# A first transform in two column tiles of 64, with the product x times v folded on VectorE alone

## The chip, the core and the metric

The kernel runs on one core of a Trainium2 chip. The metric is device time in microseconds (us) from launch to end. PE is TensorE, ACT ScalarE, DVE VectorE, POOL GpSimd; SP is the queue that issues most DMAs. 1 GB/s is a thousand bytes per us.

## What is computed

A long convolution, a gate and two MLPs in sequence, over 12,480 positions of 128 channels, all in float32:

```python
h_filt = (np.maximum(pos_emb @ w1, 0.0) @ w2) * np.exp(-0.01 * pos)[:, None]
u = x * v
y = irfft(rfft(u, n=2*S) * rfft(h_filt, n=2*S), n=2*S)[:S]      # S = 12480
a = x * y
b = np.maximum(a @ w_in, 0.0) ** 2 @ w_out                      # 128 -> 2048 -> 128
h = b @ w_in2
out = (h / (1 + np.exp(-1.702 * h))) @ w_out2
```

## The kernel before

The convolution is a transform of length 99 x 127, done as matmuls. The sequence is laid out with 99 rows on the partitions and 127 columns, and the columns are paired around the middle one: a sum and a difference of columns j and -j, 64 of each (`NJ`), so 128 values per row and channel.

*Filter stage* (`filter_stage`). PE computes the hidden layer (tile `hp`), VectorE applies relu and window (tile `r`, L264), and sum and difference go to `h`: sums on GpSimd (L268, the last on VectorE), differences on VectorE (L270).

*Product and fold* (`Inputs`). x and v come in 16 chunks of 8 channels (`load`, L196 and L197: 96 rows and 3 rows of each, so four DMAs a chunk, on SP). GpSimd multiplies x by v in two halves (L207). The sum of the paired columns (`even`, L215) is GpSimd's for even chunks and VectorE's for odd ones, the difference (`odd`, L225) VectorE's. Both fill `u`, a ring of 7 tiles.

*First transform* (`s1_step`). 16 steps over `h` fill `G`, then 32 steps over `u` fill `A`, four channels a step. PE multiplies each channel's 99 x 128 block by the cosines and sines of `cs1` (L280) into a PSUM bank, of which there are four. The lower 64 partitions (from sums) are copied as they are; the upper 64 (from differences) need real and imaginary part exchanged and one sign turned. Two steps of three are evicted by ACT (L288 to L290), the third by VectorE (L284, L286). After each step `advance` multiplies, folds and loads chunks by a table of steps (`odds`); chunk c is used in steps 2c and 2c + 1 of A.

*Around it.* After steps 6, 10, 14 and 18 of A the ACT queue writes a quarter of `G` to DRAM (`gd`, L666). From step 25 on `w2b` and the first five `m` tiles are loaded on SP (L672, L299), after steps 26 and 28 the first two pieces of `gd` are read back as `Gs` on the ACT queue (L306); these use memory that the chunks' buffers occupied. The second stage then begins with `fk` (L328), and after it the MLPs, which are most of the time.

The order on each engine is as written (`tc.manual_schedule`). A DMA's issue signals one of eight semaphores, taken in turn (`DMAHW0` to `DMAHW7`); an issue that takes a semaphore again first waits until the DMA that had it has landed.

Of the kernel before, what the change touches and what calls it, by code (L numbers as in the profile page):

```python
# [9 lines left out]
FP32 = mybir.dt.float32  # L10
# [3 lines left out]
ACTF = mybir.ActivationFunctionType  # L14
# [19 lines left out]
XC = 8  # L34
# [57 lines left out]
def conv_mlp_kernel(ctx: ExitStack, tc: tile.TileContext, xc, xt, vc, pt, w1, w2,  # L92
# [4 lines left out]
    const = ctx.enter_context(tc.tile_pool(name="const", bufs=1))  # L97
    dram = ctx.enter_context(tc.tile_pool(name="dram", bufs=1, space=bass.MemoryType.DRAM))

    cs1 = const.tile([N1, 2 * N1], FP32, name="cs1")  # L100
    ci2 = const.tile([N1, 2, N1], FP32, name="ci2")
    sign = const.tile([128, 2], FP32, name="sign")

    bd = dram.tile([2, NJ, N1, 2, D], FP32, name="bd")
    gd = dram.tile([128, N1, 2 * F], FP32, name="gd")
# [74 lines left out]
    class Inputs:  # L180


        def __init__(self, up, pool, first, early):
            self.up, self.pool, self.tiles, self.u = up, pool, {}, {}
            self.first, self.early = first, early
            self.loaded = self.done = self.odd_done = 0

        def load(self):
            c = self.loaded
            if c == NXC or c >= self.early and c - max(self.odd_done, self.early) == 3:  # L190
                return
            self.loaded += 1
            pool, bufs = (self.first, self.early) if c < self.early else (self.pool, 3)
            xs, vs = (pool.tile([N1, XC, 2, NJ], FP32, tag=n, name=n, bufs=bufs) for n in ("x", "v"))
            for r in (slice(0, ROWS), slice(ROWS, N1)):
                nc.sync.dma_start(out=xs[r], in_=xc[c, r])  # L196
                nc.sync.dma_start(out=vs[r], in_=vc[c, r])  # L197
            self.tiles[c] = xs, vs

        def multiply(self):  # L200
            c = self.done
            if c == self.loaded:
                return
            self.done += 1
            xs, vs = self.tiles[c]
            for i in range(0, XC, 4):
                nc.gpsimd.tensor_tensor(out=xs[:, i:i + 4], in0=xs[:, i:i + 4], in1=vs[:, i:i + 4],  # L207
                                        op=ALU.mult)
            self.u[c] = self.up.tile([N1, XC, 2 * NJ], FP32, tag="u", name="u", bufs=7)
            if c % 2 == 0:  # L210
                self.even(c, nc.gpsimd)

        def even(self, c, engine):
            xs, _ = self.tiles[c]
            engine.tensor_tensor(out=self.u[c][:, :, 0:NJ], in0=xs[:, :, 0], in1=xs[:, :, 1], op=ALU.add)  # L215

        def odd(self):
            c = self.odd_done
            if c == self.done:
                return  # L220
            self.odd_done += 1
            if c % 2:
                self.even(c, nc.vector)
            xs, _ = self.tiles.pop(c)
            nc.vector.tensor_tensor(out=self.u[c][:, :, NJ:2 * NJ], in0=xs[:, :, 0], in1=xs[:, :, 1],  # L225
                                    op=ALU.subtract)

    def filter_stage(fp, bank, h, inputs):

        HC = 4  # L230
        NC_ = NJ // HC
        bw1 = fp.tile([128, 128], FP32, name="bw1", bufs=1)
        warm = fp.tile([128, 1], FP32, name="warm", bufs=1)
        win = fp.tile([N1, 2, NJ], FP32, name="win", bufs=1)
        nc.vector.memset(warm, 0.0)
        p_t = {}

        def load_pos(c):
            p = fp.tile([128, HC, N1], FP32, tag="pos", name="pos", bufs=12)
            nc.sync.dma_start(out=p, in_=pt[:, c * HC:(c + 1) * HC, :])  # L240
            p_t[c] = p

        nc.scalar.dma_start(out=bw1, in_=w1)
        for c in range(12):
            load_pos(c)
        nc.scalar.dma_start(out=win, in_=c_win)
        nc.scalar.activation(out=warm, in_=warm, func=ACTF.Sigmoid)
        nc.scalar.dma_start(out=cs1, in_=c_s1)
        nc.vector.memset(sign[:, 0:1], 1.0)
        nc.vector.memset(sign[:, 1:2], -1.0)  # L250

        for j in range(0, NJ, JF):
            for c in range(j // HC + 12, min(j // HC + 12 + JF // HC, NC_)):
                load_pos(c)
            if j >= JF:
                inputs.load()
            ps = bank("hp")[:N1]
            for i in range(JF):
                nc.tensor.matmul(out=ps[:, i * 2 * F:(i + 1) * 2 * F],
                                 lhsT=p_t[(j + i) // HC][:, (j + i) % HC, :], rhs=bw1)  # L260
            r = fp.tile([N1, 2, F, JF], FP32, tag="r", name="r")
            for s in range(2):
                wb = win[:, s, j:j + JF].unsqueeze(1).to_broadcast([N1, F, JF])
                nc.vector.scalar_tensor_tensor(  # L264
                    out=r[:, s], in0=ps.rearrange("p (j s f) -> p s f j", j=JF, s=2)[:, s],
                    scalar=0.0, in1=wb, op0=ALU.max, op1=ALU.mult)
            last = j + JF == NJ
            (nc.vector if last else nc.gpsimd).tensor_tensor(  # L268
                out=h[:, :, j:j + JF], in0=r[:, 0], in1=r[:, 1], op=ALU.add)
            nc.vector.tensor_tensor(out=h[:, :, NJ + j:NJ + j + JF], in0=r[:, 0], in1=r[:, 1],  # L270
                                    op=ALU.subtract)
            if j >= NJ - 2 * JF:
                inputs.multiply()

    def s1_step(bank, src, d, dst, on_vector):


        ps = bank("s1").rearrange("p (e k) -> p e k", e=4)[:, :, 0:2 * N1]
        for e in range(4):
            nc.tensor.matmul(out=ps[:, e], lhsT=src[:, d + e, :], rhs=cs1)  # L280
        ps = ps.rearrange("p e (c k) -> p k c e", c=2)
        low, high = slice(0, NJ), slice(NJ, 128)
        if on_vector:
            nc.vector.tensor_copy(out=dst[low], in_=ps[low])  # L284
            sb = sign[high].unsqueeze(1).unsqueeze(3).to_broadcast([NJ, N1, 2, 4])
            nc.vector.tensor_tensor(out=dst[high], in0=ps[high, :, ::-1], in1=sb, op=ALU.mult)  # L286
        else:
            nc.scalar.copy(out=dst[low], in_=ps[low])  # L288
            nc.scalar.copy(out=dst[high, :, 0], in_=ps[high, :, 1])
            nc.scalar.activation(out=dst[high, :, 1], in_=ps[high, :, 0], func=ACTF.Copy, scale=-1.0)  # L290

    m_t, h_t = {}, {}

# [333 lines left out]
    with tc.manual_schedule():  # L627
# [7 lines left out]
        G = sgs.enter_context(tc.tile_pool(name="G", bufs=1, side="right")).tile(  # L635
            [128, N1, 2, F], FP32, name="G")
        vp = vps.enter_context(tc.tile_pool(name="v", bufs=3, side="right"))
        odds = {-(-12 * c // 5) + 1 for c in range(NXC)}
        steps = [0]

        def advance():
            inputs.multiply()
            if steps[0] in odds:
                inputs.odd()
            inputs.load()
            steps[0] += 1

        with tc.tile_pool(name="h", bufs=1) as hp:
            h = hp.tile([N1, F, 2 * NJ], FP32, name="h")
            inputs = Inputs(up, vp, hp, 5)  # L650
            with tc.tile_pool(name="fil", bufs=2) as fp:
                filter_stage(fp, bank, h, inputs)
            for f in range(0, F, 4):
                s1_step(bank, h, f, G[:, :, :, f:f + 4], f // 4 % 3 == 2)
                advance()
            assert inputs.odd_done >= inputs.early
        with tc.tile_pool(name="A", bufs=1, reuse_waits="tile") as ap_, ExitStack() as mps:
            A = ap_.tile([128, N1, 2, D], FP32, name="A")
            for d in range(0, D, 4):
                s1_step(bank, inputs.u[d // XC], d % XC, A[:, :, :, d:d + 4], d // 4 % 3 == 2)  # L660
                if d // 4 < 25:
                    advance()
                if d // 4 in (6, 10, 14, 18):
                    q = 25 * (d // 16 - 1)
                    q = slice(q, min(q + 25, N1))
                    nc.scalar.dma_start(out=gd[:, q], in_=G[:, q].rearrange("p k c f -> p k (c f)"))  # L666
                if d // 4 == 25:
                    assert inputs.odd_done == NXC
                    vps.close()
                    mp = mps.enter_context(tc.tile_pool(name="mh", bufs=1, reuse_waits="tile"))  # L670
                    w2b = mp.tile([128, 2 * D], FP32, name="w2b")
                    nc.sync.dma_start(out=w2b, in_=w2)  # L672
                if d // 4 in (25, 26, 27, 28, 29):
                    load_m(mp, d // 4 - 25)
                if d // 4 in (26, 28):
                    load_h(mp, (d // 4 - 26) // 2)
            sgs.close()
# [15 lines left out]
def _constants():  # L693
# [6 lines left out]
        return 2.0 * np.pi * ((num % den) / den)  # L700

    a = angle(n1[:, None] * (4 * k1[None, :] + 1), 4 * N1)
    s1 = np.concatenate([np.cos(a), -np.sin(a)], 1)
    i2 = np.stack([np.cos(a.T) / NT, -np.sin(a.T) / NT], 1)
    a = angle(j[:, None, None] * (4 * (k1[None, :, None] + N1 * k2[None, None, :]) + 1), 4 * NT)
    s2 = np.zeros((128, N1, 2, 128))
# [72 lines left out]
```

## Time and profile before

| | |
|---|---|
| median of 3 runs | 1455.44 us (1452.51 to 1455.81) |
| the profiled execution | 1450.28 us |
| its span, first to last instruction | 1448.5 us |
| granted TensorE clock, mean | 0.986 of full speed |
| PE busy | 1410.4 us (97%) |
| VectorE, ACT, GpSimd busy | 1128.7, 956.9, 278.7 us |
| chain that ended last | PE 88%, VectorE 4%, DMA 4% |

The shares are means over stages with different limits. The diff touches the first 121 us alone, so this stretch has to be read by itself. A matmul in float32 leaves two records in the trace, and a weight load (PEld) beside each.

### The profile page before, as it was taken

How to read it: one execution, taken by the hardware profiler on the slowest of the kernel's cores; microseconds unless marked ns; L12 is line 12 of the kernel's file. 1: busy time of each engine (PE TensorE's matmuls, PEld its weight loads, DVE VectorE, ACT ScalarE, POOL GpSimd, SP SyncE). 2: the span in 40 equal slices, each digit the busy share in tenths (PEclk: the TensorE clock that was granted, in tenths of full speed). 3: DMA queues.
4: the chain of work that ended last, by engine and by line, in shares of the span. 5: the costliest groups of instructions: out<-in, count | busy, mean ns of one | idle time of the engine just before them, and what ended most of it. 6: DMA issues, size and time to landing. Idle time of an engine off the chain costs nothing.

```text
span 1448.5 us, 17134 instructions
## 1 busy us (share of the span) xinstructions
PE 1410.4 (97%) x6634; PEld 1193.6 (82%) x6634; DVE 1128.7 (78%) x1241; ACT 956.9 (66%) x1117; POOL 278.7 (19%) x249
## 2 busy tenths in 40 slices
PE   7888999999999999999999999999999999999998
PEld 7877888788878888888888888888888888888887
DVE  6736898779987778777777777777787777877887
ACT  1654444376766777767676667777777667777776
POOL 7651222234622100121011210112001120000000
PEclk9999999999999999999999999999999999999999
DMA  9395776522210000100000000000000000000000
GB/s 257 90 299 176 238 245 211 180 81 78 74 37 19 26 26 8 37 19 26 17 18 30 26 26 8 26 30 27 26 8 26 30 26 8 8 8 0 15 15 14
DMA packets 46397, 91.21 MB, mean 63 GB/s; under 512 B 4183, under 2 KB 30604, under 8 KB 45804
## 3 DMA queue, kind: packets, MB, share of 16 engines
q1 hardware_dynamic: 35886, 57.17, 13.5%
q10 hardware_dynamic: 10430, 32.95, 5.9%
q8 instruction: 52, 0.85, 0.2%
q14 instruction: 29, 0.24, 0.1%
HBM read 64.25 MB, written 25.85 MB: 62 GB/s over the span
## 4 chain that ended last, share of the span: by engine, by line
PE 88%; DVE 4%; DMA 4%; issue 2%; ACT 1%; POOL 1%; SPq 0%; POOLq 0%; DVEq 0%; ACTq 0%
PE hin L512 12%; PE hin L511 12%; PE hin L513 12%; PE acc L512 12%; PE acc L511 12%; PE acc L513 12%; PE yps L469 4%; PE s L280 3%; PE hk L339 3%; PE xk L341 3%; PE ob L365 3%; PE fk L328 2%; DMA gd<-G 1%; DVE gl L549 1%; DMA m<-in_c_s_dram 1%
## 5 line engine op out<-in xcount | busy, mean ns | idle before, releaser
L549 DVE TENSOR_TENSOR gl<-g,gh 128x1004 fp32r<-128x1004 f32 (+4 forms) x400 | 491.4, 1229 | 35.1 <-ACT gh L545 34.5
L529 ACT ACTIVATE g<-hin 128x1004 f32<-128x1004 f32 (+4 forms) x200 | 201.2, 1006 | 237.9 <-PE hin L513 237.3
L511 PE MATMUL acc<-gh,w 128*128 128x502 f32 (+4 forms) x800 | 313.5, 392 | 0.4 <-DVE lo L458 0.4
L511 PE MATMUL hin<-hi,w 128*128 128x502 f32 (+4 forms) x800 | 312.7, 391 | 0.0
L512 PE MATMUL acc<-gl,w 128*128 128x502 f32 (+4 forms) x800 | 311.8, 390 | 0.8 <-DVE gl L549 0.8
L512 PE MATMUL hin<-lo,w 128*128 128x502 f32 (+4 forms) x800 | 312.3, 390 | 0.0
L513 PE MATMUL acc<-gh,w 128*128 128x502 f32 (+4 forms) x800 | 311.7, 390 | 0.0
L513 PE MATMUL hin<-hi,w 128*128 128x502 f32 (+4 forms) x800 | 311.5, 389 | 0.0
L416 POOL TENSOR_TENSOR b<-uv 99x256 f32<-99x256 f32 x127 | 159.6, 1286 | 699.0 <-DMA uv<-bd 508.5
L540 DVE TENSOR_TENSOR g<-hin,g 128x1004 f32<-128x1004 f32 (+4 forms) x200 | 238.7, 1193 | 50.6 <-ACT g L532 50.6
L538 DVE CAST gh<-g 128x1004 fp32r<-128x1004 f32 (+4 forms) x200 | 141.6, 708 | 150.8 <-ACT g L530 150.8
L532 ACT ACTIVATE g<-hin 128x1004 f32<-128x1004 f32 (+4 forms) x200 | 200.1, 1000 | 75.2 <-PE hin L513 67.2
L530 ACT ACTIVATE g<-g 128x1004 f32<-128x1004 f32 (+4 forms) x200 | 208.0, 1040 | 6.4
L545 ACT CAST gh<-g 128x1004 fp32r<-128x1004 f32 (+4 forms) x200 | 202.8, 1014 | 0.4 <-DVE g L540 0.4
L511 PEld LDWEIGHTS hin<-hi,w 128*128 128x128 f32 x800 | 151.3, 189 | 33.9 <-ACT g L529 2.4
L512 PEld LDWEIGHTS acc<-gl,w 128*128 128x128 f32 x800 | 151.0, 189 | 31.9 <-DVE gl L549 2.0
L513 PEld LDWEIGHTS hin<-hi,w 128*128 128x128 f32 x800 | 151.3, 189 | 30.7
L511 PEld LDWEIGHTS acc<-gh,w 128*128 128x128 f32 x800 | 151.1, 189 | 31.0 <-DVE lo L458 0.9
L512 PEld LDWEIGHTS hin<-lo,w 128*128 128x128 f32 x800 | 151.3, 189 | 30.6 <-issue 0.5
L513 PEld LDWEIGHTS acc<-gh,w 128*128 128x128 f32 x800 | 150.8, 189 | 30.4
L352 DVE TENSOR_TENSOR t<-xk,hc 128x512 f32<-128x512 f32 (+1 forms) x100 | 63.8, 679 | 25.8 <-PE xk L341 13.9
L469 PEld LDWEIGHTS yps<-ci,b 99*128 99x128 f32 x508 | 62.7, 196 | 8.2 <-issue 2.8
(67 smaller groups left out, 1132.5 us busy)
## 6 DMA issues: line engine op xcount, KB each, us to landing
uv<-bd SPq DMA_DIRECT2D x64, 198.0 KB
m<-in_c_s_dram SPq DMA_DIRECT2D x49, 256.0 KB
bd<-bs ACTq DMA_DIRECT2D x24, 512.0 KB
x<-in_xc_dram SPq DMA_DIRECT2D x16, 384.0 KB
v<-in_vc_dram SPq DMA_DIRECT2D x16, 384.0 KB
Gs<-gd ACTq DMA_DIRECT2D x12, 512.0 KB
gd<-G ACTq DMA_DIRECT2D x3, 1600.0 KB
raw<-in_moe_w_in_dram SPq DMA_DIRECT2D x8, 512.0 KB
```

The costliest lines, as they stand in the source:

```text
L416: engine.tensor_tensor(out=b[:, :, s, c], in0=uv[:, 0, :, c], in1=uv[:, 1, :, 1 - c], op=ALU.add if s != c else ALU.subtract)
L469: nc.tensor.matmul(out=ps[:, o:o + w], lhsT=b[:, c, :], rhs=ci2[:, c, r:r + w], start=(c == 0), stop=(c == 1))
L511: nc.tensor.matmul(out=out, lhsT=a, rhs=hl[0], start=first, stop=False)
L512: nc.tensor.matmul(out=out, lhsT=a, rhs=hl[1], start=False, stop=False)
L513: nc.tensor.matmul(out=out, lhsT=b, rhs=hl[0], start=False, stop=last)
L529: nc.scalar.activation(out=g, in_=ps, func=ACTF.Relu)
L530: nc.scalar.activation(out=g, in_=g, func=ACTF.Square)
L532: nc.scalar.activation(out=g, in_=ps, func=ACTF.Sigmoid, scale=1.702)
L538: nc.vector.tensor_copy(out=gh, in_=g)
L540: nc.vector.tensor_tensor(out=g, in0=ps, in1=g, op=ALU.mult)
L545: nc.scalar.copy(out=gh, in_=g)
L549: nc.vector.tensor_tensor(out=gl, in0=g, in1=gh.bitcast(FP32), op=ALU.subtract)
```

## The change

Each channel's matmul is cut in two: the 64 sum columns and the 64 difference columns of a channel are weights of a matmul each (`src[:, d + e, j]`), the first to output partitions 0 to 63, the second to 64 to 127. The program marks them as tiles of 128 rows by 64 columns, at columns 0 and 64. `cs1` gets a second pair of columns with exchange and sign built in, so that one ACT copy evicts all 128 partitions; VectorE evicts nothing. The product is one VectorE instruction a chunk, the two halves of the fold two more, all in `fold`; GpSimd does nothing for `u`. The table of steps changes with it: a chunk from 7 on is folded three steps of A after the ring's older tile has been used, and `w2b` and `m` are asked for from step 22 on.

```diff
-    cs1 = const.tile([N1, 2 * N1], FP32, name="cs1")
+    cs1 = const.tile([N1, 2, 2 * N1], FP32, name="cs1")
...
-            if c == NXC or c >= self.early and c - max(self.odd_done, self.early) == 3:
+            if c == NXC or c >= self.early and c - max(self.done, self.early) == 3:
...
-        def multiply(self):
+        def fold(self):
             c = self.done
             if c == self.loaded:
                 return
             self.done += 1
-            xs, vs = self.tiles[c]
-            for i in range(0, XC, 4):
-                nc.gpsimd.tensor_tensor(out=xs[:, i:i + 4], in0=xs[:, i:i + 4], in1=vs[:, i:i + 4],
-                                        op=ALU.mult)
-            self.u[c] = self.up.tile([N1, XC, 2 * NJ], FP32, tag="u", name="u", bufs=7)
-            if c % 2 == 0:
-                self.even(c, nc.gpsimd)
...
+            xs, vs = self.tiles.pop(c)
+            u = self.u[c] = self.up.tile([N1, XC, 2 * NJ], FP32, tag="u", name="u", bufs=7)
+            nc.vector.tensor_tensor(out=xs, in0=xs, in1=vs, op=ALU.mult)
+            nc.vector.tensor_tensor(out=u[:, :, 0:NJ], in0=xs[:, :, 0], in1=xs[:, :, 1], op=ALU.add)
+            nc.vector.tensor_tensor(out=u[:, :, NJ:2 * NJ], in0=xs[:, :, 0], in1=xs[:, :, 1],
                                     op=ALU.subtract)
...
-            if j >= NJ - 2 * JF:
-                inputs.multiply()
-
-    def s1_step(bank, src, d, dst, on_vector):
+
+    def s1_step(bank, src, d, dst):
...
         for e in range(4):
-            nc.tensor.matmul(out=ps[:, e], lhsT=src[:, d + e, :], rhs=cs1)
-        ps = ps.rearrange("p e (c k) -> p k c e", c=2)
-        low, high = slice(0, NJ), slice(NJ, 128)
-        if on_vector:
-            nc.vector.tensor_copy(out=dst[low], in_=ps[low])
-            sb = sign[high].unsqueeze(1).unsqueeze(3).to_broadcast([NJ, N1, 2, 4])
-            nc.vector.tensor_tensor(out=dst[high], in0=ps[high, :, ::-1], in1=sb, op=ALU.mult)
-        else:
-            nc.scalar.copy(out=dst[low], in_=ps[low])
-            nc.scalar.copy(out=dst[high, :, 0], in_=ps[high, :, 1])
-            nc.scalar.activation(out=dst[high, :, 1], in_=ps[high, :, 0], func=ACTF.Copy, scale=-1.0)
+            for half in range(2):
+                j = slice(half * NJ, (half + 1) * NJ)
+                nc.tensor.matmul(out=ps[j, e], lhsT=src[:, d + e, j], rhs=cs1[:, half])
+        nc.scalar.copy(out=dst, in_=ps.rearrange("p e (c k) -> p k c e", c=2))
...
-        odds = {-(-12 * c // 5) + 1 for c in range(NXC)}
+        folds = {max(-(-11 * c // 5) + 1, 2 * c + 4 if c >= 7 else 0) for c in range(NXC)}
...
-            inputs.multiply()
-            if steps[0] in odds:
-                inputs.odd()
+            if steps[0] in folds:
+                inputs.fold()
...
-                if d // 4 < 25:
+                if d // 4 < 22:
                     advance()
...
-                if d // 4 == 25:
-                    assert inputs.odd_done == NXC
+                if d // 4 == 22:
+                    assert inputs.done == NXC
...
-                if d // 4 in (25, 26, 27, 28, 29):
-                    load_m(mp, d // 4 - 25)
+                if 22 <= d // 4 < 27:
+                    load_m(mp, d // 4 - 22)
...
-    s1 = np.concatenate([np.cos(a), -np.sin(a)], 1)
+    s1 = np.stack([np.concatenate([np.cos(a), -np.sin(a)], 1),
+                   np.concatenate([-np.sin(a), -np.cos(a)], 1)], 1)
```

VectorE's queue from the last filter block on, first before: the folds (`u`) stand between evictions (`G<-s1`) that wait for PE.

```order
L264 SCALAR_TENSOR_TENSOR r_282<-hp_273,win_89 99x512
L268 TENSOR_TENSOR h_83<-r_282 99x64x8 [waits DVE_49]
L270 TENSOR_TENSOR h_83<-r_282 99x64x8
L225 TENSOR_TENSOR u_265<-x_143 99x8x64 [waits DMAHW5_49,DMAHW3_49,Pool_49]
L284 COPY G_76<-s1_321 64x198x4 [waits PE_49]
L286 TENSOR_TENSOR G_76<-s1_321,sign_62 64x198x4
L215 TENSOR_TENSOR u_289<-x_163 99x8x64 [waits DMAHW7_49,DMAHW1_49,Pool_49]
L225 TENSOR_TENSOR u_289<-x_163 99x8x64
L284 COPY G_76<-s1_357 64x198x4 [waits PE_49]
```

And now, at the same place (L206 to L208 are `fold`, `x_140` is chunk 0):

```order
L245 SCALAR_TENSOR_TENSOR r_275<-hp_266,win_88 99x512
L249 TENSOR_TENSOR h_82<-r_275 99x64x8 [waits DVE_49]
L251 TENSOR_TENSOR h_82<-r_275 99x64x8
L206 TENSOR_TENSOR x_140<-x_140,v_141 99x1024 [waits DMAHW5_49,DMAHW6_49,DMAHW4_49,DMAHW3_49]
L207 TENSOR_TENSOR u_307<-x_140 99x8x64 [waits DVE_49]
L208 TENSOR_TENSOR u_307<-x_140 99x8x64
L206 TENSOR_TENSOR x_160<-x_160,v_161 99x1024 [waits DMAHW2_49,DMAHW7_49,DMAHW1_49,DMAHW0_49]
L207 TENSOR_TENSOR u_341<-x_160 99x8x64 [waits DVE_49]
L208 TENSOR_TENSOR u_341<-x_160 99x8x64
```

The evictions have gone from it, and the product stands ahead of each fold.

SP's queue, before, from the last piece of chunk 9 (`x_474`, `v_475`) to the first of chunk 11 (`x_534`); `x_500` and `v_501` are chunk 10:

```order
L197 DMA v_475<-in_vc_dram 3x1024 [waits DMAHW3_49]
L196 DMA x_500<-in_xc_dram 96x1024 [waits DMAHW4_49,DVE_49,Pool_49]
L197 DMA v_501<-in_vc_dram 96x1024 [waits DMAHW5_49,DMAHW0_49]
L196 DMA x_500<-in_xc_dram 3x1024 [waits DMAHW6_49]
L197 DMA v_501<-in_vc_dram 3x1024 [waits DMAHW0_49]
L196 DMA x_534<-in_xc_dram 96x1024 [waits DMAHW1_49,DVE_49,Pool_49]
```

And now, from the last piece of chunk 8 (`v_442`) over chunk 9 (`x_481`, `v_482`) and chunk 10 (`x_526`, `v_527`) to the third piece of chunk 11 (`x_556`, `v_557`):

```order
L196 DMA v_442<-in_vc_dram 3x1024 [waits DMAHW0_49]
L195 DMA x_481<-in_xc_dram 96x1024 [waits DMAHW1_49,DVE_49]
L196 DMA v_482<-in_vc_dram 96x1024 [waits DMAHW2_49]
L195 DMA x_481<-in_xc_dram 3x1024 [waits DMAHW3_49]
L196 DMA v_482<-in_vc_dram 3x1024 [waits DMAHW4_49]
L195 DMA x_526<-in_xc_dram 96x1024 [waits DMAHW7_49,DMAHW6_49,DVE_49]
L196 DMA v_527<-in_vc_dram 96x1024 [waits DMAHW7_49]
L195 DMA x_526<-in_xc_dram 3x1024 [waits DMAHW0_49]
L196 DMA v_527<-in_vc_dram 3x1024 [waits DMAHW1_49]
L195 DMA x_556<-in_xc_dram 96x1024 [waits DMAHW2_49,DVE_49]
L196 DMA v_557<-in_vc_dram 96x1024 [waits DMAHW5_49,DMAHW4_49]
L195 DMA x_556<-in_xc_dram 3x1024 [waits DMAHW5_49]
```

The first write of `G` signals `DMAHW0` before and `DMAHW1` now (ACT's rows below). Before, the last piece of chunk 10 waited for it; now the first piece of chunk 9 does. The second write (`DMAHW7`) is waited for by chunk 10's v, the third (`DMAHW5`) by chunk 11's third piece.

ACT's queue around that first write, before:

```order
L288 COPY A_464<-s1_540 64x198x4 [waits PE_49]
L289 COPY A_464<-s1_540 64x99x4
L290 ACTIVATE A_464<-s1_540 64x99x4
L666 DMA gd_64<-G_76 128x3200 [waits DMAHW0_49,DVE_49,Activation_49]
L288 COPY A_464<-s1_552 64x198x4 [waits PE_49]
L289 COPY A_464<-s1_552 64x99x4
```

And now, to the second write:

```order
L262 COPY A_491<-s1_572 128x198x4 [waits PE_49]
L637 DMA gd_63<-G_75 128x3200 [waits DMAHW1_49,Activation_49]
L262 COPY A_491<-s1_593 128x198x4 [waits PE_49]
L262 COPY A_491<-s1_603 128x198x4 [waits PE_49]
L262 COPY A_491<-s1_623 128x198x4 [waits PE_49]
L262 COPY A_491<-s1_633 128x198x4 [waits PE_49]
L637 DMA gd_63<-G_75 128x3200 [waits DMAHW7_49]
```

One copy a step has taken the place of three instructions; the first write still follows step 6 of A, the second step 10. The end of the transform on ACT, before (from the copy of step 26, with the two reads of `Gs`):

```order
L288 COPY A_464<-s1_742 64x198x4 [waits PE_49]
L289 COPY A_464<-s1_742 64x99x4
L290 ACTIVATE A_464<-s1_742 64x99x4
L306 DMA Gs_767<-gd_64 128x1024 [waits DMAHW3_49,DMAHW5_49,DMAHW2_49,DMAHW6_49,DMAHW0_49,DMAHW7_49,DVE_49,Pool_49]
L288 COPY A_464<-s1_769 64x198x4 [waits PE_49]
L289 COPY A_464<-s1_769 64x99x4
L290 ACTIVATE A_464<-s1_769 64x99x4
L288 COPY A_464<-s1_779 64x198x4 [waits PE_49]
L289 COPY A_464<-s1_779 64x99x4
L290 ACTIVATE A_464<-s1_779 64x99x4
L306 DMA Gs_789<-gd_64 128x1024 [waits DMAHW7_49,DMAHW6_49]
L288 COPY A_464<-s1_800 64x198x4 [waits PE_49]
```

And now:

```order
L262 COPY A_491<-s1_842 128x198x4 [waits PE_49]
L278 DMA Gs_854<-gd_63 128x1024 [waits DMAHW4_49,DMAHW3_49,DMAHW5_49,DMAHW2_49,DMAHW6_49,DMAHW1_49,DMAHW7_49,DMAHW0_49,DVE_49]
L262 COPY A_491<-s1_856 128x198x4 [waits PE_49]
L262 COPY A_491<-s1_866 128x198x4 [waits PE_49]
L278 DMA Gs_876<-gd_63 128x1024 [waits DMAHW6_49,DMAHW4_49]
L262 COPY A_491<-s1_878 128x198x4 [waits PE_49]
L262 COPY A_491<-s1_888 128x198x4 [waits PE_49]
L262 COPY A_491<-s1_898 128x198x4 [waits PE_49]
L303 COPY fs_936<-fk_931 128x512 [waits DMAHW6_49,DMAHW4_49,PE_49]
```

The first `Gs` stands where it stood, but five steps' copies are behind it now, where VectorE had one of them before.

## Rows read from the trace of the kernel before

**Rows 1.** Windows: start:end, length, busy PE PEld DVE ACT POOL, PEclk, DMA share, GB/s.

```profile
14.00:38.00 24.00, 18.02 (x110) 17.84 (x109) 18.21 (x21) 6.79 (x12) 23.25 (x17) 0.86 0.98 245
...
78.00:100.00 22.00, 17.39 (x80) 16.65 (x81) 9.70 (x12) 11.34 (x21) 13.65 (x10) 0.84 1.00 330
100.00:121.00 21.00, 14.23 (x67) 12.74 (x65) 9.98 (x12) 10.83 (x20) 6.72 (x5) 0.84 0.69 210
131.00:200.00 69.00, 68.48 (x360) 61.32 (x359) 60.84 (x92) 34.55 (x60) 19.87 (x23) 1.00 0.69 230
```

**Rows 2.** Chain of waits, 64 to 122 us: start, us, what.

```profile
68.46 8.74 DMA gd<-G
...
91.81 7.11 DMA gd<-G
...
99.64 6.37 DMA v<-in_vc_dram
...
106.45 2.49 POOL x L207 x2
...
108.96 0.69 DVE u L215
109.65 0.61 DVE u L225
...
120.98 1.05 PE fk L328 x7
```

**Rows 3.** Groups by form, 20 to 125 us: count, busy us and mean ns, idle before.

```profile
L288 ACT COPY A<-s 64x792 f32<-64x792 f32 x22 | 17.9, 812 | 23.4 <-PE s L280 17.4 <-DVE u L225 5.7
...
L290 ACT ACTIVATE A<-s 64x396 f32<-64x396 f32 x22 | 10.9, 495 | 0.0
...
L286 DVE TENSOR_TENSOR A<-s,sign 64x792 f32<-64x792 f32 x10 | 9.9, 985 | 0.1
L284 DVE COPY A<-s 64x792 f32<-64x792 f32 x10 | 9.8, 975 | 6.1 <-issue 4.7 <-PE s L280 1.1
```

**Rows 4.** Timeline, 20 to 70 us, start of the transform: start, us, engine, line.

```profile
22.35 1.66 DVE L268 TENSOR_TENSOR h<-r 99x512 f32<-99x512 f32 x1
...
23.92 1.75 DVE L270 TENSOR_TENSOR h<-r 99x512 f32<-99x512 f32 x1
...
25.82 17.77 PE L280 MATMUL s<-cs,h 99*128 99x198 f32 x88 [5.98 <-DVE h L270]
...
28.83 0.81 ACT L288 COPY G<-s 64x792 f32<-64x792 f32 x1 [25.49 <-PE s L280]
...
31.47 0.81 ACT L288 COPY G<-s 64x792 f32<-64x792 f32 x1 [0.93 <-PE s L280]
```

**Rows 5.** Timeline of ACT, 66 to 72.5 us: first copies three steps apart.

```profile
68.38 0.81 ACT L288 COPY A<-s 64x792 f32<-64x792 f32 x1 [0.58 <-PE s L280]
...
72.40 0.81 ACT L288 COPY A<-s 64x792 f32<-64x792 f32 x1 [0.58 <-PE s L280]
```

**Rows 6.** The page's groups: ACT reading PSUM on 128 partitions.

```profile
L529 ACT ACTIVATE g<-hin 128x1004 f32<-128x1004 f32 (+4 forms) x200 | 201.2, 1006 | 237.9 <-PE hin L513 237.3
```

**Rows 7.** VectorE's groups by form: two inputs from SBUF on 128 partitions.

```profile
L549 DVE TENSOR_TENSOR gl<-g,gh 128x1004 fp32r<-128x1004 f32 x176 | 219.1, 1245 | 19.7 <-ACT gh L545 19.3
```

**Rows 8.** Chain of waits, 0 to 150 us: short matmuls back to back.

```profile
124.81 0.89 PE fk L328 x8
```

**Rows 9.** DMA issues, 0 to 130 us: count, KB each.

```profile
x<-in_xc_dram SPq DMA_DIRECT2D x16, 384.0 KB
...
gd<-G ACTq DMA_DIRECT2D x3, 1600.0 KB
```

**Rows 10.** Timeline of SP, 66 to 79 us: first and last piece of chunk 10.

```profile
67.99 0.32 SPq L196 DMA_DIRECT2D x<-in_xc_dram  x1
...
77.22 0.25 SPq L197 DMA_DIRECT2D v<-in_vc_dram  x1
```

**Rows 11.** Waits, 24 to 121 us: total, times, longest.

```profile
ACT A L288 <- DVE u L225: 5.7, 1, 5.7
```

More of the change, by code (lines that the diff above doesn't have):

```diff
@@ L98, in conv_mlp_kernel @@
     dram = ctx.enter_context(tc.tile_pool(name="dram", bufs=1, space=bass.MemoryType.DRAM))
-    cs1 = const.tile([N1, 2 * N1], FP32, name="cs1")
+    cs1 = const.tile([N1, 2, 2 * N1], FP32, name="cs1")
     ci2 = const.tile([N1, 2, N1], FP32, name="ci2")
-    sign = const.tile([128, 2], FP32, name="sign")
     bd = dram.tile([2, NJ, N1, 2, D], FP32, name="bd")
@@ L185, in __init__ @@
             self.first, self.early = first, early
-            self.loaded = self.done = self.odd_done = 0
+            self.loaded = self.done = 0
         def load(self):
             c = self.loaded
-            if c == NXC or c >= self.early and c - max(self.odd_done, self.early) == 3:
+            if c == NXC or c >= self.early and c - max(self.done, self.early) == 3:
                 return
@@ L204, in multiply @@
             self.done += 1
-            xs, vs = self.tiles[c]
-            for i in range(0, XC, 4):
-                nc.gpsimd.tensor_tensor(out=xs[:, i:i + 4], in0=xs[:, i:i + 4], in1=vs[:, i:i + 4],
-                                        op=ALU.mult)
-            self.u[c] = self.up.tile([N1, XC, 2 * NJ], FP32, tag="u", name="u", bufs=7)
-            if c % 2 == 0:
-                self.even(c, nc.gpsimd)
[L213 to L225, printed above, removed]
+            xs, vs = self.tiles.pop(c)
[3 more added lines that the diff above has]
+            nc.vector.tensor_tensor(out=u[:, :, NJ:2 * NJ], in0=xs[:, :, 0], in1=xs[:, :, 1],
                                     op=ALU.subtract)
@@ L248, in filter_stage @@
         nc.scalar.dma_start(out=cs1, in_=c_s1)
-        nc.vector.memset(sign[:, 0:1], 1.0)
-        nc.vector.memset(sign[:, 1:2], -1.0)
         for j in range(0, NJ, JF):
@@ L653, in conv_mlp_kernel @@
             for f in range(0, F, 4):
-                s1_step(bank, h, f, G[:, :, :, f:f + 4], f // 4 % 3 == 2)
+                s1_step(bank, h, f, G[:, :, :, f:f + 4])
                 advance()
-            assert inputs.odd_done >= inputs.early
+            assert inputs.done >= inputs.early
         with tc.tile_pool(name="A", bufs=1, reuse_waits="tile") as ap_, ExitStack() as mps:
@@ L659, in conv_mlp_kernel @@
             for d in range(0, D, 4):
-                s1_step(bank, inputs.u[d // XC], d % XC, A[:, :, :, d:d + 4], d // 4 % 3 == 2)
-                if d // 4 < 25:
+                s1_step(bank, inputs.u[d // XC], d % XC, A[:, :, :, d:d + 4])
+                if d // 4 < 22:
                     advance()
```

## The prediction

> **What bounds the kernel now.** I read the windows by stage first, for PE's busy time, clock and the share of the DMA engines; then the chain of waits over the stage that the diff touches; then that stage's groups by form. From 131 us on PE is busy 68.48 us of 69 [rows 1], in code that the change leaves alone: nothing is to be won there. From 78 to 121 us, the second half of the first transform, it is busy 17.39 of 22 us and 14.23 of 21 us, at a mean granted clock of 0.84, while the DMA engines are full (share 1.00, 330 GB/s) [rows 1]. The chain there is no arithmetic: it stands in the write of G to DRAM (8.74 and 7.11 us), in the last piece of a v (6.37 us), and after that in GpSimd's product (2.49 us) and VectorE's fold (0.69 and 0.61 us) [rows 2]. So the touched stage lasts from PE's first `s1` matmul at 25.82 us [rows 4] to `fk` at 120.98 us [rows 2]: 95.2 us for 48 steps.
>
> Where nothing waits, ACT's first copies of steps three apart start at 68.38 and 72.40 us [rows 5]: 1.34 us a step, or 167.5 ns for each of a step's 8 matmul records (an fp32 matmul leaves two). 48 such steps are 64.3 us; the other 31 us of the stage are waits and lower clock. That is all that this change can win.
>
> **The change part by part.**
>
> *Eviction.* ACT's three instructions (0.81 us, and two halves of some 0.5 us, of which the last is shown) or VectorE's two (0.98 and 0.99 us) [rows 3] become one ACT copy of 128 x 792. The trace has that copy on 64 partitions, 0.81 us [rows 3], and a 128-partition read of PSUM with 1,004 elements at 1,006 ns [rows 6], about 1 ns an element either way; bounds 0.79 and the 1.8 us that the three take now, taken 0.81. It hides behind PE's 1.34 us a step; were that cover gone, 48 copies would cost 39 us. VectorE no longer evicts, so a fold that waits for data no longer holds up an eviction queued behind it.
>
> *Product and fold.* 16 folds of one 99 x 1,024 product and two 99 x 512 operations. A VectorE operation of the same kind on 128 x 1,004 takes 1,245 ns [rows 7], the two halves 0.69 and a further 0.61 us [rows 2]: 1.25 + 0.69 + 0.61 = 2.55 us a chunk, 41 us in all, beside PE's 64 (and on the path only where PE waits for a chunk). Next to a working GpSimd such a half takes 1.75 us [rows 4], which bounds a fold at some 6.5 us; GpSimd has nothing left to do in this stage, so I take 2.55. That quiet also shortens the last two `h` operations, 1.66 and 1.75 us [rows 4], to 0.69 each: PE starts 2.0 us earlier, at 23.8 us. From then on a chunk's GpSimd time (2.49 us) is off the path.
>
> *Small things.* Two memsets go and `cs1` doubles; both lie in the filter stage, before 23.8 us; uncovered, the 77 KB more would cost 0.3 us at 245 GB/s [rows 1]. [...]
>
> *The matmuls.* 8 a step instead of 4, each with all 198 moving columns but 64 weight columns, alternately on the lower and upper half of the output partitions. No row shows such a pair. If the two halves run side by side, a step stays at 1.34 us (no less, since each record still streams 198 columns); if they run one after the other, it is 16 x 167.5 ns = 2.68 us. I take 1.34: the trace shows loads of weights running under matmuls already (8 records of 128 columns with their loads in 0.89 us [rows 8], 111 ns each), so neither load nor issue has been the limit down to that rate, and the halves share no weights and no output partition. [...]
>
> [...]
>
> *DMA.* Each chunk is 2 x 384 KB (0.8 MB with its small pieces), G's writes 1,600 KB each [rows 9], 6.5 MB in all. A DMA's issue waits for the earlier DMA that used its semaphore. Now chunk 10's first piece is issued at 67.99 us, its last only at 77.22 [rows 10], when the first write of G (issued 68.46, 8.74 us) has landed [rows 2]. In the new order chunk 9's first piece takes over the semaphore of that write, a chunk earlier; chunk 10 then has the second write's, chunk 11 the third's, chunk 13 the fourth's. On SP everything behind waits too: the later chunks, `w2b`, the `m` tiles. VectorE's fold waits for them, then PE; on VectorE only later folds stand behind.
> The first write follows step 6 of A: 23.8 + 2.7 + 23 x 1.34 + 0.8 = 58.1 us. From there 6.5 MB of G and 7 chunks (5.7 MB) must move. In the kernel before, 6.5 MB and 6 chunks (4.9 MB) took from 68.46 to 106.0 us [rows 2]: 302 GB/s. 12.2 MB at that rate are 40.3 us: the last chunk lands at 98.4 us. (330 GB/s [rows 1] would give 95, and is the low end; a wait for each write in turn is a rival.)
> Then its fold, 2.55: 101.0. The read-back `Gs` stands on ACT ahead of the last five copies and waits for the last fold: it did so before, when ACT stood 5.7 us for VectorE's fold [rows 11]. Issue 0.4, five copies 4.1, the second issue 0.4 (PE's last two steps, 2.7, lie beside these, or 5.4 at the lower clock): about 106 to 107, taken 107. Before, the same tail from the last landing took 15 us, with GpSimd's product and the lower clock in it.
>
> **Sum.** 120.98 - 107 = 14 us off. Of the profiled execution's 1450.28 us (span 1448.5 and 1.8 around it) that leaves 1436.3. Its runs' median is 1455.44, 5.2 above that execution, so I name **1441.4 us**. A measurement of this kernel tells about 0.3% (4.4 us) from no change.
>
> **Rivals.**
>
> *One after the other* (the other sign). The two halves share the 198-column stream or the issue, and PE needs 2.68 us a step. For it: no row shows two matmuls at once, and every dense stretch goes exactly by columns. Against it: different partitions of the output, different weight columns. Time: 23.8 + 2.7 + 128.6 + 1 = 156 us for `fk`, DMA far from binding: +35, 1490 us. It decides from 1.95 us a step on, where (121 - 27.5)/48 eats the whole stage.
>
> *Loads exposed.* Weights of the other half are not fetched until the matmul ahead of them has begun, so a half's matmul starts one load late. A load costs at most 111 ns for 128 columns [rows 8]; half the columns, 56 to 111. A step is then 8 x (167.5 + 56 to 111) = 1.78 to 2.23 us. At 1.78 the first write of G comes at about 67 us, the DMA work ends at 107.5 and `fk` comes at 115: 6 us won, 1449; at 2.23 PE ends at 134: 13 us lost, 1468. [...]
>
> *The chunks take it all back.* If each of the four writes must land alone before the chunk behind it moves, 4 x 8 us and 7 chunks of 3.3 us (0.8 MB at 245 GB/s, the rate while chunks alone moved [rows 1]) take 55 us from 58.1: `fk` at 121, nothing won, 1455. For it: the four held pieces. Against: the trace moves chunks beside writes at 330 GB/s [rows 1].
>
> **How the numbers follow.** Forecast 0.52 (own range 1431 to 1449: `fk` from 97 to 115), loads exposed 0.23, one after the other 0.17, chunks 0.08. The serial case and the ends of the forecast are left out: about 0.2 lie outside 1430 to 1466, which takes in all but the slowest exposed loads. Faster by over 0.3%: nearly all of the forecast and half of the exposed loads, 0.62; within 0.3%: the chunks and the middle of the exposed loads, 0.15; slower: the serial case and slow loads, 0.23.
>
> **What the profile after would show.** Two matmul records of different halves begun within one record's time, and copies 1.34 us apart, prove the tiling; 1.8 or 2.7 apart name the rival. Six or more us between the first write of G and chunk 9's issue on SP prove the held chunk; PE then waits on VectorE's folds from A's step 18 on. `fk` should start near 107 us and PE from there on run as before. Wrong would be: a step over 1.95 us, folds slower than 3 us, or PE's clock falling in the waits for chunks, which would stretch the last steps.

## The result and the profile after

| | before | after | ratio, 95% interval |
|---|---|---|---|
| median, 4 runs each | 1453.97 us | 1434.91 us (1431.45 to 1438.78) | 0.9873 (0.9838 to 0.9907) |
| repeated later, 9 and 5 runs | 1450.29 us | 1435.67 us (1433.29 to 1438.28) | 0.9889 (0.9868 to 0.9909) |
| profiled execution | 1450.28 us | 1431.45 us | |
| `fk` starts, profiled execution | 120.98 us | 105.00 us | |

The changed kernel is 1.1 to 1.3% faster. The touched stage ends 16.0 us earlier. The profiled executions differ by 18.8 us; the other 2.8 us lie behind `fk`, in code that is the same: from `fk` to the end of the span 1324.7 us against 1327.5. In the repeat it was 1330.0 us, so that part is spread between executions.

Windows of the stage after the change (columns as in [rows 1]):

```profile
24.00:45.00 21.00, 21.00 (x251) 18.03 (x252) 18.41 (x23) 12.05 (x15) 0.00 (x0) 1.00 0.91 220
45.00:55.00 10.00, 10.00 (x124) 8.59 (x122) 3.72 (x5) 5.96 (x8) 0.00 (x0) 1.00 0.01 2
55.00:60.50 5.50, 5.50 (x70) 4.73 (x68) 0.00 (x0) 3.28 (x5) 0.00 (x0) 1.00 0.71 298
60.50:70.00 9.50, 9.33 (x110) 7.73 (x106) 0.00 (x0) 5.85 (x8) 0.00 (x0) 1.00 0.91 313
70.00:80.00 10.00, 5.81 (x36) 3.79 (x38) 5.03 (x6) 2.33 (x3) 0.00 (x0) 0.83 1.02 356
80.00:90.00 10.00, 8.54 (x76) 6.20 (x74) 5.04 (x6) 3.27 (x4) 0.00 (x0) 0.83 0.92 280
90.00:98.00 8.00, 7.98 (x70) 6.27 (x68) 5.19 (x7) 2.46 (x3) 0.00 (x0) 0.79 0.83 205
```

Up to 70 us PE is busy almost without a gap, at a granted clock of 1.00. From 70 us on it waits and the granted clock falls, to 0.79 to 0.83 up to 98 us, as before (0.84 [rows 1]). The new thing stands in the second row: for 10 us the DMA engines do nothing (share 0.01) while 7 chunks and all of G are still to be moved. The timeline of SP and of ACT's first write, and SP's waits (engine, line, waited for: total, times, longest) name the reason:

```profile
42.16 0.25 SPq L196 DMA_DIRECT2D v<-in_vc_dram  x1
55.19 0.36 ACTq L637 DMA_DIRECT2D gd<-G  x1
60.49 0.32 SPq L195 DMA_DIRECT2D x<-in_xc_dram  x1
```

```profile
SPq L195 <- DMA gd<-G: 26.3, 3, 18.0
SPq L196 <- DMA gd<-G: 5.2, 1, 5.2
```

Between chunk 8's last piece (42.16 us) and chunk 9's first (60.49 us) SP stands 18.0 us for the first write of G, which ACT issues only at 55.19 us. SP waits for the other three writes too, 13.5 us in all. The chain of waits answers to [rows 2]:

```profile
23.55 42.28 PE s L261 x497
...
65.86 9.60 DMA gd<-G
...
75.78 5.66 DMA v<-in_vc_dram
...
84.46 5.82 DMA v<-in_vc_dram
...
91.00 6.72 DMA v<-in_vc_dram
...
97.84 1.23 DVE x L206
...
99.17 0.69 DVE u L207
99.86 0.61 DVE u L208
...
100.50 4.37 DMA Gs<-gd
...
105.00 1.14 PE fk L300 x8
```

Up to G's third write (65.86 us) the chain stands in PE; from there on, as before, in that write of G and in v's. GpSimd's 2.49 us [rows 2] are gone from it; the last fold takes 2.63 us from 97.84 on.

ACT's timeline, first copies and then in mid stage, answers to [rows 4, 5]:

```profile
25.65 0.82 ACT L262 COPY G<-s 128x792 f32<-128x792 f32 x1 [22.31 <-PE s L261]
26.99 0.82 ACT L262 COPY G<-s 128x792 f32<-128x792 f32 x1 [0.52 <-PE s L261]
...
51.11 0.82 ACT L262 COPY A<-s 128x792 f32<-128x792 f32 x1 [0.52 <-PE s L261]
52.45 0.82 ACT L262 COPY A<-s 128x792 f32<-128x792 f32 x1 [0.52 <-PE s L261]
```

A step takes 1.34 us with twice the matmuls. The groups by form, 20 to 105 us, answer to [rows 3, 7]:

```profile
L262 ACT COPY A<-s 128x792 f32<-128x792 f32 x32 | 25.8, 822 | 32.2 <-PE s L261 27.2 <-DVE u L208 5.0
...
L206 DVE TENSOR_TENSOR x<-x,v 99x1024 f32<-99x1024 f32 x16 | 19.6, 1222 | 31.3 <-DMA v<-in_vc_dram 31.3
L261 PEld LDWEIGHTS s<-cs,h 99*64 99x64 f32 x256 | 18.5, 137 | 6.8 <-POOL h L249 3.4 <-DVE h L251 0.3
```

One copy of 0.82 us evicts a step, and ACT waits for PE; VectorE's product takes 1.22 us and waits for data.

### The profile page after: what moved, and what is told of

It reads as the page before. It is cut to its first block, busy times and chain, and to the rows that moved or that the text cites. A ratio compares the mean times of both kernels' runs of the same rounds, so it can differ in the third digit from the quotient of the medians.

```text
span 1429.7 us, 17766 instructions
## 1 busy us (share of the span) xinstructions
PE 1403.7 (98%) x7018; PEld 1177.1 (82%) x7018; DVE 1115.9 (78%) x1233; ACT 939.9 (66%) x1066; POOL 224.8 (16%) x209
## 4 chain that ended last, share of the span: by engine, by line
PE 92%; DVE 4%; DMA 3%; ACT 1%; issue 1%; SPq 0%; DVEq 0%; ACTq 0%
PE hin L484 12%; PE hin L483 12%; PE acc L484 12%; PE hin L485 12%; PE acc L483 12%; PE acc L485 12%; PE yps L441 4%; PE s L261 3%; PE hk L311 3%; PE xk L313 3%; PE ob L337 3%; PE fk L300 2%; DMA v<-in_vc_dram 1%; DVE gl L521 1%; DMA gd<-G 1%; DVE r L245 1%
## 5 line engine op out<-in xcount | busy, mean ns | idle before, releaser
L485 PEld LDWEIGHTS hin<-hi,w 128*128 128x128 f32 x800 | 151.2, 189 | 30.7
L328 POOL TENSOR_TENSOR P<-t,t 128x256 f32<-128x256 f32 (+1 forms) x50 | 43.8, 876 | 191.4 <-DVE t L324 95.0
```

Source lines behind the costliest of these rows:

```text
L485: nc.tensor.matmul(out=out, lhsT=b, rhs=hl[0], start=False, stop=last)
```

## The experiments

Ten runs, taken in four batches; each batch has its own runs of the kernel before (medians 1449.41, 1450.29, 1449.96 and 1450.36 us). Diffs are against the changed kernel unless said otherwise.

**1. Do the two column tiles run side by side?** All matmuls on the lower tile:

```diff
-                nc.tensor.matmul(out=ps[j, e], lhsT=src[:, d + e, j], rhs=cs1[:, half])
-        nc.scalar.copy(out=dst, in_=ps.rearrange("p e (c k) -> p k c e", c=2))
+                nc.tensor.matmul(out=ps[0:NJ, e], lhsT=src[:, d + e, j], rhs=cs1[:, half])
+        for half in range(2):
+            j = slice(half * NJ, (half + 1) * NJ)
+            nc.scalar.copy(out=dst[j], in_=ps[0:NJ].rearrange("p e (c k) -> p k c e", c=2))
```

> All 8 matmuls of a step go to the lower column tile of 64 (output partitions 0 to 63, the second half's result over the first's), and two ACT copies of 64 partitions fill both halves of A from it; G is wrong in its upper half. Theory (two records run at once because they are on different tiles): here 16 records of a step follow each other 167.5 ns apart, a step takes 2.68 us, fk comes at 23.5 + 48 x 2.68 + 2 = 154 us and the time is near 1484 us. Rival (a record on 64 weight columns takes only half the time of one on 128, and two tiles have nothing to do with it): 16 records in 1.34 us within a step, steps 1.65 us apart because two copies of 0.82 us set them, and fk near 107 to 112 us, the time 1433 to 1442.

One execution: 1486.16 us, `fk` at 155.96 us. ACT's timeline:

```profile
59.34 1.64 ACT L264 COPY G<-s 64x792 f32<-64x792 f32 x2 [1.05 <-PE s L261]
62.03 1.64 ACT L264 COPY G<-s 64x792 f32<-64x792 f32 x2 [1.05 <-PE s L261]
```

2.69 us a step, and ACT waits for PE, so PE sets it: twice the 1.34 us of two tiles. The theory holds. The serial rival of the prediction is real, but belongs to one tile. Its price was right too (it named 2.68 us a step and 1490 us).

**2. Halves in turn.** The same tiles, but four matmuls on the lower, then four on the upper:

```diff
-        for e in range(4):
-            for half in range(2):
+        for half in range(2):
+            for e in range(4):
```

> The same 8 matmuls a step, but the four of the lower half first and then the four of the upper half, so that neighbours in PE's queue mostly share a column tile. Side by side, with starts in program order (my theory): a tile's 8 records run one after the other, 8 x 167.5 ns, and only the first of the other half overlaps the last of this one, so a step takes 14 x 167.5 ns = 2.35 us instead of 1.34, PE is the bound, fk starts near 137 us and the kernel takes about 1463 us. If PE picks whichever tile is free: copies stay 1.34 us apart and the time stays at 1431 to 1439 us. If the two tiles never ran at once and a record just became shorter: also 1.34 us.

One execution: 1440.4 us, `fk` at 111.09 us. ACT's timeline:

```profile
43.87 0.82 ACT L262 COPY G<-s 128x792 f32<-128x792 f32 x1 [0.63 <-PE s L261]
45.32 0.82 ACT L262 COPY G<-s 128x792 f32<-128x792 f32 x1 [0.64 <-PE s L261]
```

1.45 us a step, not 2.35: the expectation's theory failed, and "whichever tile is free" (1.34 us) comes nearest. With experiment 1 (one tile alone needs 2.69 us for the 16 records) two tiles must still work at once here. The trace agrees: 46 records stand in the window from 30 to 34 us, one every 87 ns, where on one tile they follow each other 168 ns apart. By these numbers PE begins matmuls of the other tile here ahead of ones that stand before them in the program. How it chooses, and where the 0.11 us a step go, stays open.

**3. Which part of the change won?** First the tiles and the single eviction alone, with GpSimd's product, the split fold and the table of before (the main lines, against before):

```diff
-            nc.tensor.matmul(out=ps[:, e], lhsT=src[:, d + e, :], rhs=cs1)
...
+            for half in range(2):
+                j = slice(half * NJ, (half + 1) * NJ)
+                nc.tensor.matmul(out=ps[j, e], lhsT=src[:, d + e, j], rhs=cs1[:, half])
+        nc.scalar.copy(out=dst, in_=ps.rearrange("p e (c k) -> p k c e", c=2))
```

> Only the first part of the change: two column tiles and one ACT copy a step; product and fold stay on GpSimd and VectorE with the old table. My theory, that VectorE's evictions queued behind folds were what kept the stage from its DMA bound: the first write of G comes near 56 us, the last chunk lands near 97, then GpSimd's product (2.5), the fold (1.3) and the tail (5): fk near 106 us, 1 to 2 us later than with the whole change, 1433 to 1438 us. Rival, that the move of the product to VectorE is the gain: fk at 115 us or later, 1445 us or more.

1437.18 us (4 runs), ratio 0.9914 (0.9897 to 0.9931), `fk` at 108.14 us. PE gains nothing from the tiles directly: a step takes 1.34 us before [rows 5] and after. They let one ACT copy evict all 128 partitions, and VectorE's evictions go; where PE stood before, it no longer does (windows of the kernel before, then of this run):

```profile
45.00:60.00 15.00, 11.19 (x44) 9.97 (x43) 9.76 (x9) 5.81 (x11) 8.32 (x7) 0.77 0.24 64
45.00:60.00 15.00, 15.00 (x184) 12.53 (x182) 9.30 (x6) 9.27 (x12) 12.90 (x10) 1.00 0.42 113
```

Then the other part alone, the fold with its table, on the full-width matmuls and evictions of before (again the main lines, against before):

```diff
-            for i in range(0, XC, 4):
-                nc.gpsimd.tensor_tensor(out=xs[:, i:i + 4], in0=xs[:, i:i + 4], in1=vs[:, i:i + 4],
-                                        op=ALU.mult)
...
+            nc.vector.tensor_tensor(out=xs, in0=xs, in1=vs, op=ALU.mult)
```

> Only the second part of the change: product and fold on VectorE with the new table, the old full-width matmuls and the old evictions (ACT two steps of three, VectorE the third). My theory: VectorE has, in six steps, two evictions (2 x 1.96 us) and three folds (3 x 2.5 us), 11.4 us where PE needs 8.0, so it is the bound at 1.9 us a step, and a chunk that is late stops evictions behind it: fk between 115 and 124 us, 1445 to 1455 us, within 0.5% of the kernel before. Rival, that the move of the product is the gain: fk near 106 us, 1433 to 1438 us.

1447.05 us (10 runs), ratio 0.9973 (0.9957 to 0.9988), `fk` at 119.92 us. Both times are as expected: 12.2 us of the gain are the tiles with their one copy, 2.4 us the fold, and within the spread of the runs they add up to the 14.6 us that the changed kernel won in its repeat. The end of the first run isn't as expected: its chain closes with PE's last steps (11.13 us from 97.07 on, at a granted clock of 0.65 from 80 to 100 us and 0.82 from 100 to 108), and `fk` is 2.1 us later than the 106 named.

**4. Does the held chunk cost anything?** The writes of G later, after steps 20 to 23 of A:

```diff
-                if d // 4 in (6, 10, 14, 18):
-                    q = 25 * (d // 16 - 1)
+                if d // 4 in (20, 21, 22, 23):
+                    q = 25 * (d // 4 - 20)
```

> The change, with the four writes of G after steps 20, 21, 22 and 23 of A instead of 6, 10, 14 and 18. If the held chunk 9 is what costs time (the DMA engines stand idle from 45 to 55 us because chunk 9's issue waits for the first write): chunks flow from 43 us on, PE waits for no fold before step 24 of A, VectorE's wait for v falls from 31 us to under 15, and only the writes and the read-back of G are late: they end near 92 us, Gs lands near 96, fk near 97 us, 8 us earlier, about 1424 us. If the amount of DMA work alone sets the end, it is the same amount: fk stays near 105 us.

One execution: 1433.45 us, `fk` at 107.13 us; missed by 10 us. The hold had moved with the writes. SP's waits and a window:

```profile
SPq L195 <- DMA gd<-G: 19.4, 2, 19.2
```

```profile
66.00:76.00 10.00, 10.00 (x124) 8.56 (x122) 0.97 (x2) 6.19 (x8) 0.00 (x0) 1.00 0.04 13
```

Now chunk 13 was held, and the engines idle from 66 to 76 us. Then the writes earlier:

```diff
-                if d // 4 in (6, 10, 14, 18):
-                    q = 25 * (d // 16 - 1)
+                if d // 4 in (0, 2, 4, 6):
+                    q = 25 * (d // 8)
```

> The writes of G follow steps 0, 2, 4 and 6 of A and write the same bytes, of which most steps' results are not there yet, so G is partly wrong; the order and the amount of all transfers stay. Theory (the last chunk is late because a chunk's transfer is held behind a write of G while the DMA engines stand idle): the first write goes out from about 46 us, the DMA engines have no idle stretch between 43 and 55 us, the last v lands near 89 us, the last fold ends near 91.5, fk starts at 96 to 97, 8 us before that of the changed kernel, and the time is 7 to 9 us below it. Rival 1 (the stage ends when PE has done its steps, the DMA is only what the waits are booked on): fk stays near 105 us and the time within 3 us. Rival 2 (the held chunk only moves along with the writes, as it did with late ones): a chunk is held for 5 us or more somewhere after 45 us with the DMA share below 0.5, and fk comes after 101 us.

The expectation's remark on the output is mistaken: G is complete before A's first step, and nothing is left out. 1432.63 us (5 runs), ratio 0.9874 (0.9854 to 0.9895); `fk` at 104.85 us, against 1435.67 us and 106.53 us for the changed kernel on the same chip, repeated with this expectation:

> The changed kernel once more, unchanged, beside the experiment with early writes. Expected: fk within 1.5 us of 105.0, PE's first s1 matmul at 23.5 us, and a ratio to the kernel before between 0.984 and 0.991. It also shows how much of the 2.8 us that the profiled executions differ by behind fk, in code that is the same, comes back: nothing or a different sign if it is only the spread of executions.

Rival 2 holds. ACT issues the writes at 50.45 to 58.36 us, but now chunk 7's last piece is the one that waits; SP's timeline and its waits:

```profile
36.41 0.30 SPq L195 DMA_DIRECT2D x<-in_xc_dram  x1
55.74 0.24 SPq L196 DMA_DIRECT2D v<-in_vc_dram  x1
```

```profile
SPq L196 <- DMA gd<-G: 20.5, 2, 19.0
```

SP stands 19.0 us there, with a DMA share of 0.01 from 43 to 50 us. By its numbers rival 1 would do as well (`fk` near 105 us, 3.0 us less time); the hold speaks for rival 2, and the next run decides between them. Wherever ACT's writes stood, a transfer of a later chunk had to reuse a write's semaphore, and SP came to it before the write had landed: its longest wait for `gd` was 18.0 us in the changed kernel, 19.2 with late and 19.0 with early writes. So neither run had tested the theory. What does is GpSimd's queue, which is free in this stage and whose four writes signal semaphores of their own in this program:

```diff
-                    nc.scalar.dma_start(out=gd[:, q], in_=G[:, q].rearrange("p k c f -> p k (c f)"))
+                    nc.gpsimd.dma_start(out=gd[:, q], in_=G[:, q].rearrange("p k c f -> p k (c f)"))
```

> The changed kernel with one edit: the four writes of G are issued on GpSimd's queue and not on ACT's, after the same steps 6, 10, 14 and 18 of A. They then use semaphores of their own, and in the program's order no chunk's transfer waits for a write any more; GpSimd has nothing else to do there. Theory (SP held behind the writes, with idle DMA engines, is what makes the last chunk late): no wait of SP for gd, chunks move on from 43 us with a DMA share above 0.5 in 45 to 55 us, the 12.2 MB take some 37 to 40 us from 43 to 45 us on, the last v lands by 88 us, the last fold ends by 91, fk starts at 93 to 97 us (PE's own 48 steps end near 88.7, and Gs takes 4.4 us from its issue after the last fold), and the time is 8 to 12 us below the changed kernel's, 1423 to 1428. Rival (the engines' rate or something else decides, as the early writes from ACT's queue let one think, which won 1.7 us at fk): fk at 102 us or later, time within 3 us of the changed kernel's.

1422.72 us (5 runs), ratio 0.9814 (0.9795 to 0.9833), `fk` at 95.46 us: the theory holds, and this kernel beats both. Its windows, GpSimd's timeline, and SP's longest wait:

```profile
45.00:55.00 10.00, 10.00 (x124) 10.00 (x120) 3.40 (x5) 6.20 (x8) 2.31 (x4) 1.00 0.56 205
55.00:60.00 5.00, 5.00 (x63) 5.00 (x61) 2.75 (x4) 3.07 (x4) 0.00 (x0) 1.00 1.00 378
60.00:70.00 10.00, 10.00 (x124) 10.00 (x121) 2.41 (x3) 5.94 (x8) 0.00 (x0) 1.00 1.04 415
70.00:80.00 10.00, 10.00 (x123) 10.00 (x121) 4.47 (x7) 6.25 (x8) 0.00 (x0) 1.00 0.97 248
```

```profile
49.79 2.31 POOL L637 DMA_DIRECT2D gd<-G  x4 [26.77 <-ACT G L262]
```

```profile
SPq L195 <- DVE u L208: 14.6, 5, 8.8
```

SP waits for no `gd` any more (31.5 us in the changed kernel; its longest wait is the one shown last, for folds), PE runs without a gap and at a granted clock of 1.00 from 45 to 80 us, and the last fold ends at 91.05 us. The writes didn't stay "after steps 6, 10, 14 and 18": nothing but G's last copy holds them back on GpSimd, so all four go out from 49.79 us. The same with the earlier places in the program is therefore nearly the same kernel:

> The writes of G on GpSimd's queue as in the experiment beside it, but after steps 0, 2, 4 and 6 of A (G is complete before A's first step, so nothing is left out). Theory: SP isn't held; writes and chunks share the engines from 46 us on, and as the amount is the same, the last v lands within 2 us of that with late writes: fk 92 to 97 us and the time within 3 us of it. Rival (writes ahead of the chunks delay them, so early is worse): the first wait of PE for a fold comes earlier than 70 us, and fk comes 3 us or more later than with writes after steps 6, 10, 14 and 18.

1423.61 us (4 runs), ratio 0.9819 (0.9798 to 0.9841), `fk` at 94.25 us. The run with early writes from ACT is the closest control: its first write goes out at the same time (50.45 us, the last 6.8 us later), and SP is held; 104.85 against 95.46 us puts the hold, all four writes together, at some 9 us. A faster queue isn't the reason: once nothing is held, the run with early writes moves 405 GB/s from 55 to 60 us, this one 378.

**5. Is that edit enough without the change?** The same one-word edit on the kernel before:

> The kernel before with the one edit that took 13 us off the changed kernel: the four writes of G on GpSimd's queue. It has GpSimd's products, the three evictions and 4 full-width matmuls a step as before. Theory (the hold behind the writes and the changed evictions are two separate losses, and in the kernel before the hold costs about as much): fk at 107 to 111 us, 10 to 14 us before its 121.0, time 1436 to 1440, so that without the hold the change would still be worth 12 to 16 us. Rival 1 (most of the change's gain was that the writes of G, and so the held chunks, come earlier; without the hold evictions and products hide beside PE's 64 us): fk at 97 to 102 us, time 1427 to 1431, within 8 us of the changed kernel with this edit. Rival 2 (evictions and GpSimd's products set the pace with or without the hold): fk after 115 us, time above 1444.

1445.66 us (12 runs), ratio 0.9971 (0.9957 to 0.9984), `fk` at 116.75 us: rival 2. SP's waits in the stage with the edit:

```profile
SPq L196 <- DVE u L225: 36.4, 6, 16.8
```

and the same waits in the kernel before:

```profile
SPq L196 <- DVE u L225: 30.7, 4, 15.7
SPq L197 <- DMA gd<-G: 10.3, 2, 8.1
```

and GpSimd's timeline with the edit:

```profile
78.30 2.49 POOL L207 TENSOR_TENSOR x<-x,v 99x512 f32<-99x512 f32 x2
80.73 0.73 POOL L666 DMA_DIRECT2D gd<-G  x1
```

No chunk waits for a write here, but SP waits 36.4 us for VectorE's folds to free a chunk's buffers, with the DMA share at 0.21 from 45 to 60 us. The kernel before already waited 30.7 us for folds and only 10.3 us for writes, so there was less to remove. It isn't a clean test of the hold alone: the writes stand behind products on GpSimd, and the first goes out only at 80.73 us. It does show that the edit is worth 13 us only together with the change (1435.67 to 1422.72), and under 5 us alone.

## Why the prediction was right, step by step

The named median was 1441.4 us, measured 1434.91 and 1435.67; the mechanism was the one predicted. The 16.0 us at `fk` (120.98 to 105.00) have three parts: the first write of G is issued 13.3 us earlier (68.46 to 55.19; the prediction's sum has 10.4), from there the last chunk lands 5.0 us later than before (37.5 us to 42.5; 2.8 in the sum), and the tail is 7.7 us shorter (15.0 to 7.3; 6.4 in the sum).

- **Tiles side by side, 1.34 us a step:** right, and shown by experiment 1. The rivals "one after the other" and "loads exposed" fall: copies are 1.34 us apart, and on one tile 16 records take 2.69 us, 168 ns each, the rate of 128 columns [rows 5]; the weight loads lengthen neither.
 A load's record lasts 137 ns on 64 columns, so by that record "loads exposed" was priced too low (56 to 111 ns). The third rival, "the chunks take it all back", falls too: the four pieces were held, but the stretch took 42.5 us and not 55.
 Exposed loads would have given 1.78 us a step or more, and starts in program order 2.35 us in experiment 2; the measured 1.34 and 1.45 us speak against both here. Two tiles took half the time of one: 1.34 us a step against 2.69.
- **Eviction 0.81 us, fold 2.55 us:** 0.82 and 2.63 us; the product 1.222 us, the halves 0.692 and 0.684 us over the stage, GpSimd idle.
- **PE starts at 23.8 us:** 23.55 and 23.18 us.
- **2.7 us in the sum for the first write of G (and in the serial rival's time):** mis-sized. It is the author's estimate of what the first two steps take beyond 1.34 us each, and no run shows it as a constant: the kernel before has its first two copies 2.64 us apart [rows 4], 1.3 us more than a step, and after the change the extra was 0 in the profiled execution and some 1.7 us in its repeat (below). So the first write of G came at 55.19 and 56.5 us and not at 58.1.
- **Last chunk 40.3 us after the first write, at 98.4 us:** it landed at 97.72 us, 42.5 us after the write; 2.2 us too few. That the landing itself is right within 0.7 us is in part luck: the write came 2.9 us too early for the sum. The held chunk 9 was right: it was issued 5.3 us after the write, and the 18.0 us wait of SP ended there; the sign named for it, six us or more, was set slightly too high. PE then waited from A's step 18 on (72.45 us), as named. The step treated the stretch as one of full DMA engines; the rows show shares of 0.71 to 1.02 in it.
- **Tail from there to `fk`, 8.6 us:** 7.3 us. ACT did wait 5.0 us for the last fold; its five copies lie beside the read-back of `Gs` (4.37 us), which ends last in the chain, and PE's last steps did not add to it.
- **From the execution to the median, 5.2 us:** 3.5 us measured. With the 2.0 us at `fk` and the 2.8 us of spread behind it this is the whole difference of 6.5 us.
- **PE's clock in the waits,** named as what could make it wrong, did fall (0.79 to 0.83 from 70 to 98 us) and stretched the steps there, PE being busy 7.98 of 8 us from 90 to 98 us. The chain shows no cost of it at `fk`: from 65.86 to 104.87 us it has no PE.

What the prediction took as given and the experiments undid: that the DMA work can only begin at the first write of G. Its reading that the DMA engines are full holds from 78 to 100 us (share 1.00); from 100 to 121 us its own row has 0.69, and from 45 to 60 us, of which it has no row, the share was 0.24 in the kernel before. Of the 31 us of waits and lower clock that it named as all that can be won, most were there for the taking: with the writes on a queue of their own `fk` came 25.5 us earlier (120.98 to 95.46), 1.9 us of it by PE's earlier start (25.82 to 23.96).

## What to carry to other kernels

Where a stage's DMA engines are full at its end, look for a stretch where they stand idle earlier, and ask which semaphore the next transfer's issue is waiting for: it can belong to another queue's transfer that merely comes earlier in the program, as here, where SP stood 18.0 us for a write of ACT's queue, 10 us of it at a DMA share of 0.01. Moving that transfer in time moved the hold along (19.2 and 19.0 us); giving it a queue with semaphores of its own removed it here, for 13 us. And two edits can be worth more than their sum, when each alone leaves the other's wait as the bound: here 14.6 and 4.7 us alone, 27.2 us together.

## What the runs showed of the hardware that was not expected

The granted clock after nearly the same idle time differed between two executions of one program. PE stood 3.27 us before its first `s1` matmul in the profiled execution of after and 3.34 us in its repeat; in the first the granted clock stayed at 1.00, in the repeat it fell to 0.50 for some 3 us. Windows of the repeat:

```profile
24.00:26.00 2.00, 2.00 (x20) 1.56 (x18) 1.97 (x3) 0.29 (x1) 0.00 (x0) 0.67 1.03 231
26.00:28.00 2.00, 2.00 (x16) 1.48 (x14) 1.97 (x4) 0.53 (x1) 0.00 (x0) 0.50 1.05 234
28.00:30.00 2.00, 2.00 (x26) 1.66 (x26) 1.97 (x3) 1.18 (x2) 0.00 (x0) 0.98 1.03 231
```

Its first two copies are 2.59 us apart (25.71 and 28.30), against 1.34 in the first execution. In the seven other profiled executions with these narrow tiles, after 3.27 to 4.39 us of idle time, it fell as well, to 0.50 to 0.52 in a window of 2 us, four of them after the same 3.27 us. By the first copies the lower clock cost nothing in the one execution and 1.7 to 2.7 us in the five others that have the same steps. A term for a lower clock in the first steps is therefore a spread here and not a constant; what decides it stays open.
